# Transposing the feed-forward activations on VectorE and by SBUF to SBUF transfers instead of on TensorE

## The chip, the cores and the metric

The kernel runs on one core of one Trainium2 chip. The time is the device time of one execution in microseconds (us). The kernel before takes 1112.11 us, the median of 3 runs (1111.66 to 1112.41).

## The reference

The first half is attention with normalised queries and keys, over 8 batches, 12 heads, 448 positions and 64 elements per head:

```python
q_n, k_n = rmsnorm(q, g_q), rmsnorm(k, g_k)      # (8, 12, 448, 64)
scores = q_n @ k_n^T / sqrt(64)
attn = exp(scores - max) / (sum + 1e-9)
x = (attn @ v) as (8*448, 12*64)                 # 3584 tokens, 768 wide
```

The second half is a feed-forward block with the SoLU activation and a layer norm:

```python
h = x @ w_in                                     # 768 -> 1024
solu = h * softmax(h)
ln = (solu - mean) / sqrt(var + 1e-6) * g_ln
out = ln @ w_out                                 # 1024 -> 768
```

All is float32, and the two weights arrive as float64 and are converted in the kernel.

## The kernel before, in words

Only `fast_path` runs on these inputs (`general_path`, its twin for large gains, is compiled and skipped). Attention goes by pairs of heads: 8 batches x 6 pairs are 48 steps, n = 0 to 47. The feed-forward goes by tiles of 128 tokens: 28 tiles, t = 0 to 27. The two run interleaved: tile t can begin when the attention of its tokens is done.

What a step n issues, in this order: the loads of pair n+4 (L505, eight transfers on SP, each 32 partitions by 14 pieces of 128 B), the squares of pair n+3, two of the four key chunks of the scores (`s`, L572) with their exponentials (`E`, L576), the transpose of q and k of pair n+1 on VectorE (`qkT`, L559), the norm of pair n+2 (`ss` L529, `nx`, `ny`, and `qkn` on GpSimd, L549), the product with the values of pair n-1 (`o`, L595), the load of v for pair n+1 (L514), the sums of pair n-1 (`sm`, L604, with `es`, the added exponentials), and the last two chunks of scores. `divide` (L617 to L621) turns `o` and `sm` into `xT`, the transposed input of the feed-forward.

What a tile issues: `ff_in` in two halves (`h`, L635, 6 matmuls of 512 columns each), then `ff_max`, `ff_moments` and `ff_norm` (L645 to L667), which leave the normalised activation `u` (128 tokens by 1024), then `ff_transpose`, which needs `u` with the 1024 features on partitions (`uT`, 8 blocks of 128x128), and `ff_out` in two halves (`po`, L686, 8 matmuls of 384 columns each), whose result is copied to `y` (L687) and stored (L689, on ScalarE's queue). `ff_transpose` runs four tiles after the `ff_in` of its tile, so `u` is ready long before.

The order is written out by hand: within `tc.manual_schedule()` every engine executes its instructions in the order in which the program issues them. Pieces of work are called through `unit`, which counts them and lets pieces that were put off by `later` follow one, two or three units on. The feed-forward's pieces stand in the list `events`, for each tile in the order

```python
events += [a, c, b, d, e]    # ff_in(t, 0), ff_transpose(t-4), ff_in(t, 1), ff_out(t-4, 0), ff_out(t-4, 1)
```

and a step takes up to five of them, when the attention is far enough: `ff(0)` after the second chunk of scores, `ff(1)` after `sums`, `ff(2)` after the fourth chunk. The list is not aligned to the steps, so where `ff_transpose` falls changes in the course of the kernel: in tiles 0 to 12 it stands in `ff(0)`, ahead of the values and sums, in tiles 13 to 19 in `ff(1)`, just behind the sums. After the last step the remaining pieces follow without attention work between them; the last four tiles are `ff_transpose`, `ff_out`, `ff_out` four times over.

Weights are converted during the first 22 steps (`convert_w`, the buffer `tmp`); its buffers shared a tag with `uT` (two buffers), so one took the place of the other.

Buffers: `work` and `loads` have two unless said otherwise (`qk` three, `v` three, `u` five), PSUM has one buffer `h` of two banks and six of one bank. SP issues all loads, in program order; a transfer that waits for a buffer holds up those behind it.

Of the kernel before, what the change touches and what calls it, by code (L numbers as in the profile page):

```python
# [9 lines left out]
FP32 = mybir.dt.float32  # L10
U32 = mybir.dt.uint32
# [355 lines left out]
def fast_path(  # L367
# [16 lines left out]
    nc = tc.nc  # L384
    B, H, S, D = q.shape
    DM, DFF = moe_w_in.shape
    P = 128
    NJ = 4
    SP = S // NJ
    NB = S // 32  # L390
    NP = H // 2
    KD = DM // P
    KF = DFF // P
# [6 lines left out]
    loads = ctx.enter_context(tc.tile_pool(name="loads", bufs=2))  # L400
    work = ctx.enter_context(tc.tile_pool(name="work", bufs=2))
    small = ctx.enter_context(tc.tile_pool(name="small", bufs=4))
    ps_h = ctx.enter_context(tc.tile_pool(name="ps_h", bufs=1, space=bass.MemoryType.PSUM))
    ps_t = ctx.enter_context(tc.tile_pool(name="ps_t", bufs=6, space=bass.MemoryType.PSUM))

    ident = consts.tile([P, P], FP32, name="ident")
# [3 lines left out]
    w_out = consts.tile([P, KF, DM], FP32, name="w_out")  # L410
# [46 lines left out]
    def convert_w(step, raw):  # L457

        _, dst, c, cols = step
        n = cols.stop - cols.start  # L460
        lo, hi = raw[:, :, 0], raw[:, :, 1]
        tmp = work.tile([P, 2, n], U32, tag="uT", name="tmp")
        e, m = tmp[:, 0], tmp[:, 1].bitcast(FP32)
        ei = e.bitcast(I32)

        def fields():
            nc.vector.tensor_scalar(tmp[:, 1], hi, 0xFFFFF, None, OP.bitwise_and)  # L467
            nc.vector.tensor_scalar(e, hi, 20, 0x7FF, OP.logical_shift_right, OP.bitwise_and)

        def scale():  # L470
            nc.scalar.activation(m, tmp[:, 1], AF.Copy, scale=2.0 ** -20, bias=1.0)
            nc.scalar.activation(ei, ei, AF.Relu, bias=m896)

        def join():
            nc.vector.scalar_tensor_tensor(m, lo, 2.0 ** -52, m, OP.mult, OP.add)  # L475
            nc.vector.tensor_scalar(ei, ei, 255.0, 2.0 ** 23, OP.min, OP.mult)
            nc.vector.scalar_tensor_tensor(e, hi, 0x80000000, e, OP.bitwise_and, OP.bitwise_or)  # L477

        def product():
            if dst is w_in:  # L480
                nc.gpsimd.tensor_tensor(dst[:, c, cols], m, e.bitcast(FP32), OP.mult)
            else:

                nc.vector.scalar_tensor_tensor(
                    dst[:, c, cols], m, gcol[:, c : c + 1], e.bitcast(FP32), OP.mult, OP.mult
                )

        return [fields, scale, join, product]
# [21 lines left out]
    def load_v(n):  # L510
        b, hp = divmod(n, NP)
        d = st[n]
        d["v"] = loads.tile([SP, 2, NJ, D], FP32, tag="v", name="v", bufs=3)
        nc.sync.dma_start(d["v"], v[b, 2 * hp : 2 * hp + 2].rearrange("h (j p) d -> p h j d", j=NJ))  # L514

    def squares(n):
# [83 lines left out]
    def sums(n):  # L600
        d = st[n]
        d["sm"] = ps_t.tile([P, S], FP32, tag="t", name="sm")
        for h in range(2):
            nc.tensor.matmul(  # L604
                d["sm"][h * D : (h + 1) * D, :], ones[0:SP, :], d["es"][:, h], start=True, stop=True
            )
        later(1, lambda: divide(n))

    def divide(n):

        b, hp = divmod(n, NP)
        d = st[n]
        if b // 2 not in xTs:
            xTs[b // 2] = work.tile([P, KD, 2 * S], FP32, tag="xT", name="xT")
        r = work.tile([P, NB, 32], FP32, tag="r", name="r")
        rc = small.tile([P, NB], FP32, tag="rc", name="rc")
        nc.vector.transpose(r.rearrange("p b i -> p (b i)"), d["sm"])  # L617
        nc.vector.reciprocal(rc, r[:, :, 0])
        nc.vector.transpose(r, rc.rearrange("p b -> p b ()").to_broadcast([P, NB, 32]))  # L619
        c0 = (b % 2) * S  # L620
        nc.vector.tensor_tensor(xTs[b // 2][:, hp, c0 : c0 + S], d["o"], r.rearrange("d b i -> d (b i)"), OP.mult)  # L621
        del st[n]
# [5 lines left out]
    def ff_in(t, half):  # L628
        m, i = divmod(t, 2 * S // P)
        d = mt.setdefault(t, {})  # L630
        if half == 0:
            d["h"] = ps_h.tile([P, DFF], FP32, tag="h", name="h")
        hs = slice(half * 512, half * 512 + 512)
        for c in range(KD):
            nc.tensor.matmul(  # L635
                d["h"][:, hs], xTs[m][:, c, i * P : (i + 1) * P], w_in[:, c, hs], start=(c == 0), stop=(c == KD - 1)
            )
# [29 lines left out]
        nc.vector.tensor_scalar(d["u"], d["u"], d["mv"][:, 0:1], d["e"], OP.subtract, OP.mult)  # L667

    def ff_transpose(t):
        d = mt[t]  # L670
        d["uT"] = work.tile([P, KF, P], FP32, tag="uT", name="uT")
        for half in range(2):
            pt = ps_t.tile([P, 4, P], FP32, tag="t", name="pu")
            for i in range(4):
                c = 4 * half + i
                nc.tensor.transpose(pt[:, i], d["u"][:, c * P : (c + 1) * P], ident)  # L676
            (nc.vector.tensor_copy if half else nc.scalar.copy)(d["uT"][:, 4 * half : 4 * half + 4], pt)  # L677

    def ff_out(t, half):
        d = mt[t]  # L680
        if half == 0:
            d["y"] = work.tile([P, DM], FP32, tag="y", name="y")
        hs = slice(half * HO, (half + 1) * HO)
        po = ps_t.tile([P, HO], FP32, tag="t", name="po")
        for c in range(KF):
            nc.tensor.matmul(po, d["uT"][:, c], w_out[:, c, hs], start=(c == 0), stop=(c == KF - 1))  # L686
        nc.scalar.copy(d["y"][:, hs], po)  # L687
        if half == 1:
            nc.scalar.dma_start(out[t * P : (t + 1) * P, :], d["y"])  # L689
            del mt[t]  # L690
# [37 lines left out]
    def feed():  # L728

        nonlocal wdone  # L730
        for c in list(stages):
            c.pop(0)()
            if len(c) == 1 and len(raws) < len(wq):
                raws.append(load_w(wq[len(raws)]))
            if not c:
                stages.remove(c)
        if wdone < min(wtarget, len(wq)) and len(stages) < 2 and not (stages and len(stages[-1]) > 2):
            stages.append(convert_w(wq[wdone], raws[wdone]))
            wdone += 1
# [5 lines left out]
    def second(t, a, b):  # L745
        return [(W_OUT + 1, lambda: ff_transpose(t)), a, (W_OUT + 1, lambda: ff_out(t, 0)), b, (W_OUT + 1, lambda: ff_out(t, 1))]

    nothing = (0, None)
    for t in range(NT):
        ready = -(-(t + 1) * P // S) * NP + 1  # L750
        a = (max(ready, W_IN + 1), lambda t=t: ff_in(t, 0))
        b = (max(ready, W_IN + 1), lambda t=t: ff_in2(t))
        waiting.append(t)
        if len(waiting) > (LAG if t < NT - 8 else 1):
            c, _, d, _, e = second(waiting.pop(0), nothing, nothing)
# [11 lines left out]
    load(0)  # L767
    setup()
    load_v(0)
    raws.append(load_w(wq[0]))  # L770
    load(1)
    raws.append(load_w(wq[1]))
    load(2)
    load_v(1)
    with tc.manual_schedule():
        prepare(0)
# [17 lines left out]
        for n in range(N):  # L794
# [38 lines left out]
            if n and n + 1 < N:  # L833
                load_v(n + 1)
# [87 lines left out]
```

## Time and profile before

| | |
|---|---|
| median of 3 runs | 1112.11 us |
| profiled execution | 1109.11 us, of it 1107.3 us span from first to last instruction |
| TensorE matmuls (PE) | 1035.3 us busy, 93% |
| TensorE weight loads (PEld, beside PE) | 475.6 us, 43% |
| VectorE (DVE) | 605.4 us, 55% |
| ScalarE (ACT) | 370.6 us, 33% |
| GpSimd (POOL) | 240.3 us, 22% |
| transfers, SP's queue (q1) | 225984 packets, 45.64 MB, 20.9% of 16 engines |
| granted TensorE clock, mean | 0.981 |

How to read it: the page gives for each group of instructions the line, the engine, the operation and the tiles (output <- inputs), the count, the busy time, the mean of one in ns, and the idle time just before with what ended it. The chain of work that ended last is followed back from the last instruction, so it tells what the end waited for. In a timeline a row has the start and the length in us; rows of the same kind are merged, and in square brackets stands how long the engine was idle before and who released it. Matmuls overlap each other, so the length of one record is not what it costs; the chain and the starts of neighbours give that. An fp32 matmul has two records.

### The profile page before, as it was taken

The page shows a single profiled execution, that of the slowest core. Times are in us where ns is not written, and L with a number is a line of the kernel's source. Part 1 is how long each engine was busy: PE and PEld are TensorE (multiplying, and loading weights), DVE is VectorE, ACT ScalarE, POOL GpSimd, SP SyncE. Part 2 cuts the span into 40 slices and gives each one's busy share as a digit, 9 for nine tenths or more (in the row PEclk, how much of TensorE's full clock was granted, in tenths as well). Part 3 has the DMA queues.
Part 4 walks back from the last instruction along what each step waited for, and adds up shares of the span by engine and source line. Part 5 has one row for each costly group of instructions (what it writes and reads, how often), then busy time and mean ns, then how long its engine had stood idle before and what let it go on. Part 6 is the DMA issues. An engine that isn't in the chain of part 4 may idle for free.

```text
span 1107.3 us, 10659 instructions
## 1 busy us (share of the span) xinstructions
PE 1035.3 (93%) x3617; PEld 475.6 (43%) x3617; DVE 605.4 (55%) x1018; ACT 370.6 (33%) x773; POOL 240.3 (22%) x155
## 2 busy tenths in 40 slices
PE   3988888888789999999999999999999999999997
PEld 1323233333234444444444444444444444455554
DVE  3999996569997444444444444454446644522300
ACT  3656553235564222222222222332224322311110
POOL 2565651123223111111111011121112211100000
PEclk9899999998989999999999999999999999999999
DMA  7454544014543111111111111121111100000010
GB/s 140 89 122 98 124 87 85 23 39 93 112 88 62 40 40 40 39 32 33 32 37 40 40 40 39 40 51 40 40 39 40 34 23 24 14 15 15 15 44 31
DMA packets 230391, 57.49 MB, mean 52 GB/s; under 512 B 223152, under 2 KB 223160, under 8 KB 230328
## 3 DMA queue, kind: packets, MB, share of 16 engines
q1 hardware_dynamic: 225984, 45.64, 20.9%
q10 hardware_dynamic: 4344, 11.08, 2.6%
q8 instruction: 30, 0.49, 0.2%
q14 instruction: 33, 0.27, 0.1%
HBM read 45.68 MB, written 11.01 MB: 51 GB/s over the span
## 4 chain that ended last, share of the span: by engine, by line
PE 75%; DVE 14%; issue 4%; ACT 3%; DMA 1%; SPq 1%; ACTq 0%; DVEq 0%
PE po L686 27%; PE h L635 26%; PE s L572 9%; PE o L595 9%; DVE es L586 2%; PE pu L676 2%; PE sm L604 2%; DVE tmp L467 2%; DVE qkT L559 2%; DVE tmp L475 1%; SPq L505 1%; DVE r L619 1%; DVE tmp L477 1%; DVE r L617 1%; PE ss L529 1%
## 5 line engine op out<-in xcount | busy, mean ns | idle before, releaser
L635 PE MATMUL h<-w_in,xT 128*128 128x512 f32 x672 | 305.0, 604 | 11.7 <-DVE u L653 11.7
L686 PE MATMUL po<-w_out,uT 128*128 128x384 f32 x896 | 298.0, 489 | 2.9 <-ACT uT L677 2.9
L686 PEld LDWEIGHTS po<-w_out,uT 128*128 128x128 f32 x896 | 168.3, 190 | 132.9 <-issue 15.0
L572 PE MATMUL s<-qkT 64*112 64x448 f32 x768 | 204.6, 584 | 16.9 <-ACT E L576 6.7
L576 ACT ACTIVATE E<-s 112x448 f32<-112x448 f32 x384 | 178.0, 550 | 110.0 <-PE s L572 109.9
L635 PEld LDWEIGHTS h<-w_in,xT 128*128 128x128 f32 x672 | 126.2, 193 | 167.5 <-issue 162.8
L584 POOL TENSOR_TENSOR es<-E 112x896 f32<-112x896 f32 x48 | 110.5, 2301 | 325.2 <-ACT E L576 318.7
L595 PE MATMUL o<-E,v 112*64 112x448 f32 x768 | 163.9, 572 | 1.2 <-DVE xT L621 1.2
L572 PEld LDWEIGHTS s<-qkT 64*112 64x112 f32 x768 | 76.6, 177 | 136.9 <-issue 73.6
L677 DVE COPY uT<-pu 128x512 f32<-128x512 f32 x28 | 19.2, 687 | 187.3 <-PE pu L676 187.3
L586 DVE TENSOR_TENSOR es<-es,E 112x896 f32<-112x896 f32 x96 | 115.1, 1199 | 10.9 <-ACT E L576 7.8
L663 POOL TENSOR_TENSOR he<-he,mhalf 128x1 f32<-128x1 f32 x28 | 21.7, 774 | 379.2 <-DVE he L662 379.2
L549 POOL TENSOR_TENSOR qkn<-qk,ny 128x896 f32<-128x896 f32 x48 | 83.0, 1730 | 81.6 <-DVE ny L544 35.0
L648 ACT ACTIVATE u<-h,hmax 128x1024 f32<-128x1024 f32 x28 | 31.2, 1114 | 207.3 <-DVE hmax L645 207.3
L687 ACT COPY y<-po 128x384 f32<-128x384 f32 x56 | 26.8, 479 | 213.5 <-PE po L686 213.5
L595 PEld LDWEIGHTS o<-E,v 112*64 112x64 f32 x768 | 53.2, 143 | 86.5 <-issue 80.5
L645 DVE TENSOR_REDUCE hmax<-h 128x1 f32<-128x1024 f32 x28 | 34.3, 1224 | 84.3 <-PE h L635 84.3
L604 PE MATMUL sm<-es,ones 112*64 112x448 f32 x192 | 44.8, 544 | 16.0 <-DVE es L586 14.1
L617 DVE STREAM_TRANSPOSE r<-sm 128x448 f32<-128x448 f32 x48 | 31.0, 646 | 45.8 <-PE sm L604 45.8
L524 DVE TENSOR_REDUCE part<-sq 128x28 f32<-128x896 f32 x48 | 51.7, 1076 | 5.9 <-ACT sq L519 5.9
L519 ACT ACTIVATE sq<-qk 128x896 f32<-128x896 f32 x48 | 45.8, 955 | 23.1 <-ACT y L687 11.3
L559 DVE STREAM_TRANSPOSE qkT<-qkn 128x896 f32<-128x896 f32 x48 | 52.9, 1102 | 0.0
(54 smaller groups left out, 578.7 us busy)
## 6 DMA issues: line engine op xcount, KB each, us to landing
qk<-in_q_dram SPq DMA_DIRECT2D x192, 56.0 KB, 2.6
qk<-in_k_dram SPq DMA_DIRECT2D x192, 56.0 KB, 2.4
v<-in_v_dram SPq DMA_DIRECT2D x48, 224.0 KB, 3.0
out_dram<-y ACTq DMA_DIRECT2D x28, 384.0 KB, 2.3
raw<-in_moe_w_in_dram SPq DMA_DIRECT2D x12, 512.0 KB, 4.2
raw<-in_moe_w_out_dram SPq DMA_DIRECT2D x16, 384.0 KB, 3.4
grow<-in_g_q_dram ACTq DMA_DIRECT2D x2, 0.2 KB
grow<-in_g_k_dram ACTq DMA_DIRECT2D x2, 0.2 KB
```

Source lines behind the costliest of these rows:

```text
L519: nc.scalar.activation(d["sq"], d["qk"].rearrange("p s b d -> p (s b) d"), AF.Square)
L524: nc.vector.tensor_reduce(d["part"], d["sq"], AX, OP.add)
L549: nc.gpsimd.tensor_tensor(d["qkn"], d["qk"].rearrange("p s b d -> p (s b) d"), d["y"].rearrange("p b -> p b ()").to_broadcast([P, 2 * NB, ...
L559: nc.vector.transpose(d["qkT"].rearrange("p s t -> p (s t)"), d["qkn"].rearrange("p b d -> p (b d)"))
L572: nc.tensor.matmul(s, d["qkT"][hh, 1, kc * SP : (kc + 1) * SP], d["qkT"][hh, 0, :], start=True, stop=True)
L576: nc.scalar.activation(d["E"][:, kc, h], d["s", h], AF.Exp)
L584: nc.gpsimd.tensor_tensor(d["es"], d["E"][:, 0], d["E"][:, 1], OP.add)
L586: nc.vector.tensor_tensor(d["es"], d["es"], d["E"][:, kc], OP.add)
L595: nc.tensor.matmul(d["o"][h * D : (h + 1) * D, :], d["v"][:, h, kc], d["E"][:, kc, h], start=(kc == 0), stop=(kc == NJ - 1),)
L604: nc.tensor.matmul(d["sm"][h * D : (h + 1) * D, :], ones[0:SP, :], d["es"][:, h], start=True, stop=True)
L635: nc.tensor.matmul(d["h"][:, hs], xTs[m][:, c, i * P : (i + 1) * P], w_in[:, c, hs], start=(c == 0), stop=(c == KD - 1))
L686: nc.tensor.matmul(po, d["uT"][:, c], w_out[:, c, hs], start=(c == 0), stop=(c == KF - 1))
```

## The change

`ff_transpose` no longer uses TensorE. VectorE transposes `u` in 32x32 blocks into a new buffer `ub`: each block is transposed where it lies, so the features of a block land on the 32 partitions of its token group. Sixteen transfers on SP then move them: from partition group a (tokens) of `ub` to partition group m (features) of `uT`, each 32 partitions by 8 pieces of 128 B, 32 KB. The eight transposes a tile, their two PSUM tiles and the two copies to SBUF go. The place of `ff_transpose` in the list of events is the same.

To make room, `ub` shares the tag `tmp` with the weight conversion, `uT` has its own, and three buffer counts go down: `v` from three to two, `r` and `y` from two to one. `ff_out` reads the same data of `uT` in the new shape.

```diff
@@ convert_w
-        tmp = work.tile([P, 2, n], U32, tag="uT", name="tmp")
+        tmp = work.tile([P, 2, n], U32, tag="tmp", name="tmp")
@@ load_v
-        d["v"] = loads.tile([SP, 2, NJ, D], FP32, tag="v", name="v", bufs=3)
+        d["v"] = loads.tile([SP, 2, NJ, D], FP32, tag="v", name="v", bufs=2)
@@ divide
-        r = work.tile([P, NB, 32], FP32, tag="r", name="r")
+        r = work.tile([P, NB, 32], FP32, tag="r", name="r", bufs=1)
@@ ff_transpose
         d = mt[t]
-        d["uT"] = work.tile([P, KF, P], FP32, tag="uT", name="uT")
-        for half in range(2):
-            pt = ps_t.tile([P, 4, P], FP32, tag="t", name="pu")
-            for i in range(4):
-                c = 4 * half + i
-                nc.tensor.transpose(pt[:, i], d["u"][:, c * P : (c + 1) * P], ident)
-            (nc.vector.tensor_copy if half else nc.scalar.copy)(d["uT"][:, 4 * half : 4 * half + 4], pt)
+        ub = work.tile([P, KF, 4, 32], FP32, tag="tmp", name="ub")
+        d["uT"] = work.tile([P, KF, 4, 32], FP32, tag="uT", name="uT")
+        nc.vector.transpose(ub.rearrange("p c m t -> p (c m t)"), d["u"])
+        for a in range(4):
+            for m in range(4):
+                nc.sync.dma_start(
+                    d["uT"][m * 32 : m * 32 + 32, :, a], ub[a * 32 : a * 32 + 32, :, m]
+                )
@@ ff_out
-            d["y"] = work.tile([P, DM], FP32, tag="y", name="y")
+            d["y"] = work.tile([P, DM], FP32, tag="y", name="y", bufs=1)
@@
-            nc.tensor.matmul(po, d["uT"][:, c], w_out[:, c, hs], start=(c == 0), stop=(c == KF - 1))
+            nc.tensor.matmul(po, d["uT"][:, c].rearrange("p a t -> p (a t)"), w_out[:, c, hs], start=(c == 0), stop=(c == KF - 1))
```

## Prediction

> **What bounds the kernel now.** I read the busy table first, then the chain of work that ended last, then the timelines around the change. The page:
>
> ```profile
> span 1107.3 us, 10659 instructions
> PE 1035.3 (93%) x3617; PEld 475.6 (43%) x3617; DVE 605.4 (55%) x1018; ACT 370.6 (33%) x773; POOL 240.3 (22%) x155
> ...
> PE po L686 27%; PE h L635 26%; PE s L572 9%; PE o L595 9%; DVE es L586 2%; PE pu L676 2%; PE sm L604 2%; DVE tmp L467 2%; DVE qkT L559 2%; DVE tmp L475 1%; SPq L505 1%; DVE r L619 1%; DVE tmp L477 1%; DVE r L617 1%; PE ss L529 1%
> ...
> L677 DVE COPY uT<-pu 128x512 f32<-128x512 f32 x28 | 19.2, 687 | 187.3 <-PE pu L676 187.3
> ...
> qk<-in_q_dram SPq DMA_DIRECT2D x192, 56.0 KB, 2.6
> ```
>
> TensorE is the limit: once the feed-forward runs (from about 340 us) there is next to no gap on it. The transposes (pu, L676) hold 2% of the chain, about 22 to 28 us; that is all the change can win. VectorE waits 187 us in front of its copy L677, so there is room on it, but the groups don't say when. So I looked tile by tile: where can VectorE begin the new transpose, and when does TensorE want uT for po (L686)? VectorE runs in order, so the start is where the copy L677 stands, without its wait for pu. The 28 tiles fall into four kinds. A tile of the first kind (tile 8), VectorE's timeline:
>
> ```profile
> 577.27 0.69 DVE L677 COPY uT<-pu 128x512 f32<-128x512 f32 x1 [9.86 <-PE pu L676]
> ```
>
> VectorE had been free for 9.86 us, since 567.41; po of this tile starts at 586.33. Slack 18.9 us. It is so for tiles 1 to 12 (18.3 to 20.7). A tile of the second kind (tile 13), first VectorE's timeline, then the chain:
>
> ```profile
> 737.78 0.62 DVE L621 TENSOR_TENSOR xT<-o,r 128x448 f32<-128x448 f32 x1
> 738.32 0.68 DVE L677 COPY uT<-pu 128x512 f32<-128x512 f32 x1
> ```
> ```profile
> 735.34 0.75 PE sm L604 x4
> 736.10 1.02 PE pu L676 x8
> 737.12 5.15 PE h L635 x12
> 742.27 1.69 PE s L572 x8
> 743.96 1.17 PE po L686 x3
> ```
>
> Here the copy waits for no pu: it stands behind xT (L621), which hangs on sm. VectorE can begin at 738.32, and the timeline starts po at 743.89: slack 5.6 us. It is the same in tiles 13 to 19. This is the place that decides. Tile 0 has 7.7 us, tile 20 has 9.0, tiles 21 to 23 have 14. The last four have no other work between their transposes and po; TensorE's timeline:
>
> ```profile
> 1052.35 1.04 PE L676 MATMUL pu<-ident,u 128*128 128x128 f32 x8
> 1054.08 10.59 PE L686 MATMUL po<-w_out,uT 128*128 128x384 f32 x32 [0.69 <-ACT uT L677]
> 1064.50 1.04 PE L676 MATMUL pu<-ident,u 128*128 128x128 f32 x8
> 1066.23 10.59 PE L686 MATMUL po<-w_out,uT 128*128 128x384 f32 x32 [0.69 <-ACT uT L677]
> ```
>
> 12.2 us per tile, 1.6 of them for pu and the copy.
>
> How dear a burst of transfers on SP is, its timeline shows at one pair's loads (eight transfers of 32 partitions by 14 pieces of 128 B; the new ones are 32 by 8 pieces of 128 B):
>
> ```profile
> 732.74 1.88 SPq L505 DMA_DIRECT2D qk<-in_q_dram  x4
> 734.65 2.05 SPq L505 DMA_DIRECT2D qk<-in_k_dram  x4
> ```
>
> Issues are in series: 0.36 us to the second, then 0.52 from one to the next.
>
> **The Trainium skill.** "VectorE: DVE Perf Modes", section "The three transpose paths", says that VectorE transposes 32x32 blocks each by itself and not 128x128 at once; hence the 16 transfers. The trace gives the price: 1102 ns for 128x896 (L559). "DMA: Bandwidth & Descriptors", section "Issuing engines are not separate DMA queues", calls the time to start a DMA "usually small relative to the DMA itself". The trace disagrees for this size: 16 issues at about 0.5 us are 8 us beside 2.4 us from issue to landing. Its section "Rules for kernel authors" says that under 64 KB one pays mostly overhead. The trace agrees: a 56 KB load lands in 2.4 us though its 448 packets take 448 x 12.5 ns / 16 = 0.35 us of sixteen engines.
>
> **The change part by part.**
>
> Removed from TensorE: 8 transposes a tile. Their records say 273 ns each, but they overlap; the chain gives 0.91 us a tile in tiles 1 to 12 (1.02 in 13 to 19, 0.87 in 21 to 23). Removed from ScalarE and VectorE: the copies (0.59 and 0.69 us a tile), both off the path outside the last four tiles.
>
> Added, from the start on VectorE to po, call it X:
> - Transpose of 128x1024: 1.102 x 1024/896 = 1.26 us. Its waits for the transfers that last read the buffer ub (two buffers, so those of two tiles before, long done): 0.1, an estimate; 0 to 0.4.
> - Hand over to SP: 0.03 to 0.05 (POOL's qkn ends at 581.66, SP issues at 581.69).
> - 16 issues: 0.36 + 14 x 0.50 = 7.36 us to the start of the last. The pitch: issues behind a transfer with 448 pieces come at 0.52, behind one with 896 at 0.60 (v at 17.58, next at 18.18); so 0.50 for 256. Bounds: 0.36 for each (5.4) and 0.52 plus one wait for a semaphore (8.2).
> - Landing of the last: no SBUF to SBUF transfer is in the trace. Loads take 1.7 at least, 2.4 in the median; I take 2.1, bounds 1.6 and 2.6.
> - TensorE's po waits for eight DMA semaphores: 0.1, bounds 0 and 0.3.
> X = 1.26 + 0.1 + 0.05 + 7.36 + 2.1 + 0.1 = 11.0 us; bounds 8.4 and 12.4.
>
> What lies on the path:
> - Tiles 1 to 12: 11.0 is under 18.9, hidden by o, sm and h; gain 12 x 0.91 = 10.9. If that cover were gone each would cost as below.
> - Tiles 13 to 19: 738.32 + 11.0 = 749.32 against 743.89: 5.4 later, 7 x 5.4 = +38.0. TensorE has no other idle time in these steps to give it back (29.0 of 29.0 us busy between 732 and 761), and what follows on it is ready.
> - Tile 0: 342.18 + 11.0 = 353.2 against 349.92: +3.3. Tile 20: 968.56 + 11.0 = 979.6 against 977.54: +2.0.
> - Tiles 21 to 23: 11.0 under 14.1; gain 3 x 0.87 = 2.6.
> - Tile 24: VectorE free at 1049.4, so po at 1060.4 against 1054.08: +6.35. Tiles 25 to 27: po back to back at 10.55 instead of 12.2: -1.65 x 3 = -4.95. Their uT has two buffers: transfers for tile 26 start when po of 24 ends, and 0.05 + 7.36 + 2.1 + 0.1 = 9.6 is under 10.5, just hidden. Sum +1.4.
> Total: -10.9 + 38.0 + 3.3 + 2.0 - 2.6 + 1.4 = +31.2 us.
>
> Queues. On SP the 16 issues stand behind the pair's loads (and v in tiles 13 to 19), which wait for POOL's qkn and for o of the pair before last; both are done before VectorE ends (735.3 for o, 739.6 for VectorE in tile 13). Behind them the next pair's loads wait: from 732.7 to about 747.5 in tile 13; squares needs them in the step after next, near 785, so nothing. The listing of the new kernel's instructions with their waits shows that every transfer, the stores on ACT too, takes one of eight semaphores in turn and waits for its last user: eight issues are 4.0 us and a landing is 2.4, so no wait; in tiles 24, 26 and 27 one transfer waits for the store of an earlier tile (out of 23 lands near 1055.4, the 13th issue is near 1056.7). v with two buffers, r and y with one: v is reloaded after o two pairs earlier, a step ahead of use; r is used by VectorE in order; y's store lands 2.3 us after issue, under the 5.2 us to the next copy. All nothing, at worst 2 us. VectorE gets 28 x 1.26 instead of 28 x 0.69: 16 us more, in its idle time. Transfers: 28 x 4096 packets x 12.5 ns / 16 = 90 us of the sixteen engines, 8% on 23%.
>
> The profiled execution took 1109.11 (span 1107.3 and 1.8 around it), 3.0 below the median 1112.11. With +31.2 it would be 1140.3, and the median 1143.3.
>
> **Rivals.**
> (a) The burst is cheaper. This is the one that ends faster. Each tile of 13 to 19 pays X - 5.57, tile 0 X - 7.74, the tail X - 9.6, against 13.5 gained elsewhere and 0.7 in tile 20: the sign turns at X = 7.8 us. For: some issues take only 0.31 and the fastest landing is 1.7. Against: in every burst of loads the third and later issues come at 0.52; X = 7.8 would need 16 issues at 0.31 throughout. At X = 7.2 the sum is 11.4 - 0.5 - 0.7 - 2.4 - 13.5 = -5.7: 1106.4. Near that point, X = 7.8: 1112.
> (b) Bound by bound, X = 8.4 to 9.5: 7 x 2.9 to 7 x 3.9 and the rest give +5 to +16: 1117 to 1128.
> (c) SBUF to SBUF pieces of 128 B move slowly and set the pitch at about 0.8: X = 16. Tiles 13 to 19 +73, tiles 0 and 20 +15, tiles 21 to 23 +5, the tail +13, less 10.9: +95, 1207. Against: loads of the same piece size take 12.5 ns a packet. For: nothing in the trace, it just has no such transfer.
> (d) Everything is hidden, gain 27 us, 1085: would need VectorE to start tiles 13 to 19 before xT, and its order forbids it. No chance worth a number.
>
> **How the numbers follow.** Likeliest case (X of 9.5 to 12.4) 0.80: 1143, its own range 1128 to 1160. (b) 0.05, (c) 0.08, (a) 0.07, of which 0.02 within 0.2% of the median (about what a measurement of this kernel can tell from no change) and 0.05 faster. Slower is 0.80 + 0.05 + 0.08 = 0.93. The range takes the likeliest case and part of (b): 1120 to 1160.
>
> **What would show it.** In the new profile: idle time of TensorE before po released by a DMA on uT, some 6 us in each of tiles 13 to 19 (5.4 and the 1.02 that pu no longer takes), 4 in tile 0, 3 in tile 20, 8 in tile 24, none in tiles 1 to 12; the VectorE transpose at 1.26 us; 16 issues spread over 7 to 8 us; landings near 2.1. It is wrong if the issues come at 0.36, if SP holds the burst back behind a load or v, or if TensorE waits for uT in tiles 1 to 12.

## The result and the profile after

The changed kernel takes 1190.89 us (median of 4 runs, 1188.48 to 1193.74) against 1112.05 for the kernel before in the same runs: ratio 1.071, 95% interval [1.0685, 1.0735]. It is slower by 79 us, where 31 were forecast; it lies above the forecast's range of 1120 to 1160. The profiled execution took 1193.74 us, of it a span of 1191.9.

The page of the kernel after, with the busy row of TensorE, its granted clock over the span in 40 slices (9 is full), the chain by line, po's group (busy, mean ns, then idle time before it), and the new transfers (count, KB each, us from issue to landing):

```profile
span 1191.9 us, 10860 instructions
...
PE 1039.0 (87%) x3393; PEld 465.6 (39%) x3393; DVE 626.7 (53%) x1018; ACT 355.3 (30%) x745; POOL 240.4 (20%) x155
...
PEclk9999998987898999999999999888989888989989
...
PE po L689 25%; PE h L635 23%; PE o L595 7%; PE s L572 7%; SPq L678 5%; DVE es L586 3%; DVE qkT L559 2%; PE sm L604 2%; DVE tmp L467 2%; DVE r L619 1%; SPq L505 1%; DVE r L617 1%; DVE tmp L475 1%; DMA uT<-ub 1%; DVE hmax L645 1%
...
L689 PE MATMUL po<-w_out,uT 128*128 128x384 f32 x896 | 323.1, 521 | 84.0 <-DVE qkT L559 42.7
...
uT<-ub SPq DMA_DIRECT2D x448, 32.0 KB, 1.9
```

The clock row and po's group of the kernel before, for comparison:

```profile
PEclk9899999998989999999999999999999999999999
L686 PE MATMUL po<-w_out,uT 128*128 128x384 f32 x896 | 298.0, 489 | 2.9 <-ACT uT L677 2.9
```

Three things are new. The issues on SP (SPq L678) stand on the chain with 5%. TensorE is idle for 84 us before po, where it was 3. And po's matmuls, which are the same, are longer: 521 ns in the mean against 489, and the clock row falls to 8 again and again in the second half, where it stayed at 9 before; e4 below shows that these two belong together. (The page names qkT as what ended most of the idle time; at tile 13 that instruction had ended at 753.75, 0.2 us before po, and has nothing to do with po. Of the nine semaphores that po waits for, the page names one; the DMAs are the late ones, as the experiments show.)

Tile 13, the kind that decides, on TensorE in the kernel before, and then on TensorE, VectorE and SP in the changed kernel:

```profile
743.89 10.59 PE L686 MATMUL po<-w_out,uT 128*128 128x384 f32 x32
```
```profile
743.61 1.76 PE L572 MATMUL s<-qkT 64*112 64x448 f32 x8
753.95 12.77 PE L689 MATMUL po<-w_out,uT 128*128 128x384 f32 x32 [8.57 <-DVE qkT L559]
```
```profile
740.02 0.62 DVE L621 TENSOR_TENSOR xT<-o,r 128x448 f32<-128x448 f32 x1
740.75 1.25 DVE L675 STREAM_TRANSPOSE ub<-u 128x1024 f32<-128x1024 f32 x1
```
```profile
742.02 10.39 SPq L678 DMA_DIRECT2D uT<-ub  x16
752.52 2.10 SPq L505 DMA_DIRECT2D qk<-in_q_dram  x4
```

VectorE starts at 740.75, po at 753.95: X, the time from the start on VectorE to po, is 13.2 us, not 11.0. Of these 10.39 are the sixteen issues. The last issue alone takes 0.61, so the pitch (the time from one issue to the next) is (10.39 - 0.61) / 15 = 0.65 us. Then po takes 12.77 us for the 32 records that took 10.59 before. A stretch of the kernel before in the same place, then one of the changed kernel:

```profile
732.00:761.00 29.00, 29.00 (x102) 14.06 (x102) 12.68 (x22) 8.13 (x17) 4.13 (x3) 1.00 0.18 41
```
```profile
740.00:780.00 40.00, 31.43 (x96) 14.51 (x95) 14.72 (x23) 7.54 (x16) 5.12 (x3) 0.87 0.20 41
```

(columns: stretch, length, busy time of PE, PEld, DVE, ACT, POOL, granted clock, DMA share, GB/s). The clock is 0.87, where it was 1.00. In tile 8, of the covered kind, TensorE goes from h to po without a gap:

```profile
586.95 5.42 PE L635 MATMUL h<-w_in,xT 128*128 128x512 f32 x12
592.20 5.32 PE L689 MATMUL po<-w_out,uT 128*128 128x384 f32 x16
```

Where the time came from, by the start of sm (L604) of each pair in the traces, and for the last row to the end of the last po, each against the kernel before, in us. The last column is experiment e4, explained below:

| stretch | forecast | after | e4, the waits filled |
|---|---|---|---|
| before the first transpose of u | 0 | +2.2 | +3.9 |
| tile 0 (pair 22 to 23) | +3.3 | +10.0 | +5.9 |
| tiles 1 to 12 (pair 23 to 34, 11 steps) | -10.0 | -10.0 | -10.0 |
| tiles 13 to 19, seven steps | +38.0 | +69.8 | +53.7 |
| tiles 20 to 27 | +0.8 | +13.7 | +8.7 |

(The forecast's -10.9 is 12 tiles; 11 of them lie between these marks.)

### The profile page after: what moved, and what is told of

It is laid out like the page before. It is cut to its first block, busy times and chain, and to the rows that moved or that the text cites. A ratio compares the mean times of both kernels' runs of the same rounds, so it can differ in the third digit from the quotient of the medians.

```text
span 1191.9 us, 10860 instructions
## 1 busy us (share of the span) xinstructions
PE 1039.0 (87%) x3393; PEld 465.6 (39%) x3393; DVE 626.7 (53%) x1018; ACT 355.3 (30%) x745; POOL 240.4 (20%) x155
## 4 chain that ended last, share of the span: by engine, by line
PE 65%; DVE 18%; issue 6%; SPq 6%; ACT 2%; DMA 1%; POOL 1%; ACTq 0%; DVEq 0%; POOLq 0%
PE po L689 25%; PE h L635 23%; PE o L595 7%; PE s L572 7%; SPq L678 5%; DVE es L586 3%; DVE qkT L559 2%; PE sm L604 2%; DVE tmp L467 2%; DVE r L619 1%; SPq L505 1%; DVE r L617 1%; DVE tmp L475 1%; DMA uT<-ub 1%; DVE hmax L645 1%
## 5 line engine op out<-in xcount | busy, mean ns | idle before, releaser
L689 PE MATMUL po<-w_out,uT 128*128 128x384 f32 x896 | 323.1, 521 | 84.0 <-DVE qkT L559 42.7
L689 PEld LDWEIGHTS po<-w_out,uT 128*128 128x128 f32 x896 | 180.7, 204 | 229.2 <-issue 65.2
L537 DVE TENSOR_SCALAR nx<-ss 128x28 f32<-128x28 f32 x48 | 8.7, 182 | 243.5 <-ACT ny L536 243.5
L604 PE MATMUL sm<-es,ones 112*64 112x448 f32 x192 | 44.9, 544 | 16.5 <-DVE es L586 14.5
```

Of the source, the lines that this page charges most:

```text
L604: nc.tensor.matmul(d["sm"][h * D : (h + 1) * D, :], ones[0:SP, :], d["es"][:, h], start=True, stop=True)
L689: nc.tensor.matmul(po, d["uT"][:, c].rearrange("p a t -> p (a t)"), w_out[:, c, hs], start=(c == 0), stop=(c == KF - 1))
```

## The experiments

My theory after the result, A: the price is sixteen issues in series on SP, which the order of the events leaves uncovered (no other work of TensorE hides them) in tiles 0, 13 to 20 and 24 on. Rival B: the price is moving 128 B pieces within SBUF, whoever issues them. And C, for the longer matmuls: the wait itself makes the clock fall.

**e1, half of the issues on ScalarE's queue.**

```diff
-                nc.sync.dma_start(
+                (nc.scalar if m % 2 else nc.sync).dma_start(
```

> The changed kernel, with every second of the sixteen transfers issued on ScalarE's queue instead of SP's; all data still move. Theory A (the issues in series on SP are the cost: 0.65 us each, 16 in a row): 8 issues take 5.2 us instead of 10.4, X in tiles 13 to 19 falls from 13.2 to about 8.2, TensorE's wait there from 8.5 to about 3.5 us, and with the shorter waits the half-clock spells go too: about 1125 us. Theory B (moving 128 B pieces from SBUF to SBUF is the cost, whoever issues): X stays near 13 and the time near 1190.

Measured: 1168.97 us, ratio 1.0504 [1.0483, 1.0524]. In tiles 13 to 19 issues, X and waits are as A has them. SP's timeline and VectorE's start at tile 13, then TensorE's at tiles 13 to 15:

```profile
739.77 5.17 SPq L678 DMA_DIRECT2D uT<-ub  x8
```
```profile
738.50 1.25 DVE L675 STREAM_TRANSPOSE ub<-u 128x1024 f32<-128x1024 f32 x1
```
```profile
746.96 10.56 PE L689 MATMUL po<-w_out,uT 128*128 128x384 f32 x32 [3.84 <-DMA qk<-in_q_dram]
779.14 12.25 PE L689 MATMUL po<-w_out,uT 128*128 128x384 f32 x32 [3.41 <-DMA uT<-ub]
813.10 12.25 PE L689 MATMUL po<-w_out,uT 128*128 128x384 f32 x32 [3.50 <-DMA uT<-ub]
```

The same bytes in the same pieces, and X is 8.5 us (738.50 to 746.96): B falls. (The load of q that the page names for the first wait is not read by po; it is a name as misleading as qkT above.) The seven steps cost 28 us instead of 70. The time of 1125 was missed elsewhere: the last tiles cost 33.6 us. ScalarE runs in order, so there its eight issues stand behind the copies of y and the store of the tile before, and each po waits again:

```profile
1098.29 0.48 ACT L690 COPY y<-po 128x384 f32<-128x384 f32 x1 [4.68 <-PE po L689]
1098.80 0.34 ACTq L692 DMA_DIRECT2D out_dram<-y  x1
1099.33 5.94 ACTq L678 DMA_DIRECT2D uT<-ub  x8
```

The three po above also show the edge of C, and a second part of the miss: I had expected the spells of half clock to go with the shorter waits. Of the seven waits of 3.4 to 3.8 us in tiles 13 to 19 five are still followed by a spell of 3.4 us at half clock and a po of about 12.25 us, two are not (10.56).

**e2, pieces of 1 KB instead of 128 B.**

```diff
-        ub = work.tile([P, KF, 4, 32], FP32, tag="tmp", name="ub")
-        d["uT"] = work.tile([P, KF, 4, 32], FP32, tag="uT", name="uT")
-        nc.vector.transpose(ub.rearrange("p c m t -> p (c m t)"), d["u"])
+        ub = work.tile([P, 4, 32, KF], FP32, tag="tmp", name="ub")
+        d["uT"] = work.tile([P, 4, 32, KF], FP32, tag="uT", name="uT")
+        nc.vector.transpose(ub.rearrange("p m t c -> p c m t"), d["u"].rearrange("p (c m t) -> p c m t", m=4, t=32))
...
```

> The changed kernel with the free dimensions of ub and uT reordered so that each of the sixteen transfers has 32 pieces of 1 KB instead of 256 of 128 B; same bytes, same result. TensorE then loads its weights with a stride of 32 B, which may cost by itself. If the pitch of 0.65 us is a price per transfer between SBUF partitions (theory A, fixed), it stays at 0.65 and X near 13. If it follows the number of pieces (theory A, by pieces), it falls towards 0.45 and X towards 10, the time towards 1145 to 1160. If moving the pieces is the cost (theory B), the landing of 1.9 us gets shorter as well.

Measured: 1199.01 us, ratio 1.0771 [1.0753, 1.0789]. SP at tile 13:

```profile
744.11 10.01 SPq L678 DMA_DIRECT2D uT<-ub  x16
```

The pitch is 0.63 us with an eighth of the pieces, and the landing stays at 1.9: it is not the pieces. The 8 us more fit the strides, though no run takes these alone: VectorE's transpose takes about 2.0 us instead of 1.2 when it writes with a stride, and a weight load of po 313 ns instead of 190.

**e3, the smaller buffers alone, with the transposes of before.**

```diff
-        d["v"] = loads.tile([SP, 2, NJ, D], FP32, tag="v", name="v", bufs=3)
+        d["v"] = loads.tile([SP, 2, NJ, D], FP32, tag="v", name="v", bufs=2)
-        r = work.tile([P, NB, 32], FP32, tag="r", name="r")
+        r = work.tile([P, NB, 32], FP32, tag="r", name="r", bufs=1)
-            d["y"] = work.tile([P, DM], FP32, tag="y", name="y")
+            d["y"] = work.tile([P, DM], FP32, tag="y", name="y", bufs=1)
```

> The kernel before (TensorE transposes) with only the three smaller buffer counts of the change: v two, r one, y one. The changed kernel was about 2 us late before the first transpose of u. If the buffers are the cause: 1114 us, the loss before 340 us. If not: 1112 us, within 1.

Measured: 1112.2 us, ratio 0.999 [0.9978, 1.0002]: the buffers cost nothing that the medians show. Its profiled execution was 4.6 us late at pair 22, with the median unchanged, and e7 below, which has all buffers of before, was 3.4 late there. The start of the kernel differs by some us between executions, so the +2.2 of the first row of the table need not be an effect of the change.

**e4, the waits filled with matmuls of no use.**

```diff
+        fill = {0: 8, 20: 5, 24: 10}.get(t, 9 if 13 <= t <= 19 else 0)
+        if half == 0 and fill:
+            pf = ps_t.tile([P, 512], FP32, tag="t", name="pf")
+            for i in range(fill):
+                nc.tensor.matmul(pf, w_in[:, 0, 0:P], w_in[:, 1, 0:512], start=True, stop=True)
```

> The changed kernel with matmuls of no use put on TensorE just ahead of po in tiles 0, 13 to 19, 20 and 24 (8, 9, 5 and 10 of 512 columns, about 0.86 us each), so that the wait for uT is filled with work. Transfers and order are unchanged. Theory C (the wait of over 8 us halves the granted TensorE clock for 7 to 10 us, which makes po 2.3 us longer each time): the half-clock spells in tiles 13 to 19 go, each of these steps is 7.6 us longer than before instead of 9.98, and the time falls by about 20 us to 1170. Rival (these 2.35 us a step are part of the wait itself): the time stays at 1190.

Measured: 1169.91 us, ratio 1.0515 [1.0497, 1.0533], 21 us faster for 172 more matmul records. TensorE at tile 13:

```profile
742.85 7.99 PE L691 MATMUL pf<-w_in 128*128 128x512 f32 x18
751.53 10.56 PE L694 MATMUL po<-w_out,uT 128*128 128x384 f32 x32 [0.69 <-DVE qkT L559]
```
```profile
742.00:780.00 38.00, 37.31 (x118) 16.75 (x114) 14.69 (x23) 7.63 (x17) 5.11 (x3) 1.00 0.22 44
```

po is back at 10.56 us, the clock in the stretch is 1.00, and each of the seven steps is 7.4 to 7.8 us longer than before, which is X minus slack, 13.2 - 5.6 = 7.6. C holds: 16 of the 70 us of tiles 13 to 19 are the clock. The clock records of the changed kernel give the same by another way: in these seven tiles 32.6 us of half clock fall on po, and half of that is 16.3.

**e5, the transpose of each tile one tile ahead.**

```diff
-            events += [a, c, b, d, e]
+            ahead = second(waiting[0], nothing, nothing)[0]
+            events += ([a, c, b] if t == LAG else [a, b]) + [d, e, ahead]
...
-    for t in waiting:
-        events += [x for x in second(t, nothing, nothing) if x[1]]
+    for i, t in enumerate(waiting):
+        _, _, d, _, e = second(t, nothing, nothing)
+        ahead = [second(waiting[i + 1], nothing, nothing)[0]] if i + 1 < len(waiting) else []
+        events += ahead + [d, e]
```

> The changed kernel with ff_transpose of each tile moved one tile ahead in the list of events: behind ff_out of the tile before, so that VectorE's transpose and the sixteen transfers have a whole tile's work to hide behind. Nothing else is changed. Theory A (the latency X of 13.2 us from VectorE's start to po, in places where the order gives it only 5 to 9 us): no wait of TensorE for uT and no half-clock spells in tiles 0 to 23, 24 x 0.91 = 22 us less than the kernel before in that part; in the last four tiles the transfers (16 x 0.65 + 1.9 + about 0.2 = 12.5 us) are longer than po (10.5), so there about 12.5 us a tile against 12.2 before, and somewhat more where a transfer waits for the semaphore of a store: 1092 to 1098 us. Rival (the transfers cost TensorE something of their own, by sharing SBUF or by po's eight semaphore waits): above 1112.

Measured: 1114.58 us, ratio 1.0025 [1.0015, 1.0035]. 76 us are gone without a transfer less: the latency stayed, its cover came. But the sum is not A's 1092 to 1098; by the number alone it falls on the rival's side (above 1112). The steps speak against the rival: the seven that cost 70 us now gain 0.83 us each against the kernel before. What is lost is lost in three places. Two were not foreseen and are seen more plainly in e6. The third is the last four tiles, which lose 7.4 us where about 1 was expected, with waits as in the changed kernel:

```profile
1062.46 23.08 PE L689 MATMUL po<-w_out,uT 128*128 128x384 f32 x64 [9.85 <-DMA uT<-ub]
```

**e6, as e5, with tiles 24 to 27 transposed on TensorE.**

```diff
...
+        if t >= NT - 4:
+            uT = d["uT"].rearrange("p c a t -> p c (a t)")
+            for half in range(2):
...
+                    nc.tensor.transpose(pt[:, i], d["u"][:, c * P : (c + 1) * P], ident)
...
+            return
```

> As e5, but tiles 24 to 27, which have no other work to hide behind, are transposed on TensorE as in the kernel before, one tile ahead. Theory A: tiles 0 to 23 gain 22 us as in e5, the last four gain the 0.7 us that po waited for the copies: about 1087 us, below both kernels. Rival as for e5: above 1112.

Measured: 1105.0 us, ratio 0.994 [0.9924, 0.9955]. That is 0.6% below the kernel before, but 18 us above the expectation. One loss is tile 0, which the edit had left in its old place (6.7 us). The other lies at pairs 40 to 42, in steps that have no feed-forward work. SP, ScalarE and TensorE there:

```profile
841.12 10.71 SPq L687 DMA_DIRECT2D uT<-ub  x16
851.96 2.08 SPq L505 DMA_DIRECT2D qk<-in_q_dram  x4
854.09 2.04 SPq L505 DMA_DIRECT2D qk<-in_k_dram  x4
```
```profile
858.11 0.95 ACT L519 ACTIVATE sq<-qk 128x896 f32<-128x896 f32 x1 [6.66 <-DMA qk<-in_k_dram]
858.97 1.83 ACT L576 ACTIVATE E<-s 112x448 f32<-112x448 f32 x4
```
```profile
859.54 1.76 PE L604 MATMUL sm<-es,ones 112*64 112x448 f32 x4 [3.60 <-ACT E L576]
```

The burst of tile 17 holds SP for 10.7 us, the loads of q and k behind it come late, ScalarE waits 6.66 us for them in front of its squares, the exponentials stand behind the squares, and TensorE waits. In a step of 29 us the loads have time; in one of 8 to 14 us they have none.

**e7, the control: the kernel before with the same move.** The edit is that of e5 on the old transposes.

> The control for e5 and e6: the kernel before, TensorE transposes and all, with the same move of ff_transpose one tile ahead. If the gain of e5 and e6 comes from taking the transposes off TensorE, this one stays near 1112, less about 3 us for the waits of po in the last four tiles: 1109. If the move itself is what gains, it comes down as far as e6, 1087.

Measured: 1109.48 us, ratio 0.9969 [0.9958, 0.998], as expected: the move by itself gains 3 us, and not the 25 that would bring it to 1087.

**e8, the source in HBM.**

```diff
-                    d["uT"][m * 32 : m * 32 + 32, :, a], ub[a * 32 : a * 32 + 32, :, m]
+                    d["uT"][m * 32 : m * 32 + 32, :, a], q[a, m].rearrange("(b t) (x d) -> x t b d", t=32, x=2)[0][:, 0:KF]
```

> The changed kernel with the source of the sixteen transfers replaced by a piece of q in HBM, of the same shape (32 partitions by 8 pieces of 128 B); VectorE still transposes into ub, but what it leaves there is not used, so the output is not the reference's. Only the pitch of the issues is asked. If the 0.65 us comes from the source being SBUF, the pitch falls to the 0.52 of the loads of q and k or a little below. If it comes from the count of issues in a row, or from the destination, it stays at 0.65.

SP's timeline in a tile of the covered kind (one execution):

```profile
472.01 7.87 SPq L678 DMA_DIRECT2D uT<-in_q_dram  x16
```

(7.87 - 0.45) / 15 = 0.495 us from issue to issue. With the same shape and destination, the SBUF source makes it 0.65. Over all 448 issues the median of one is 0.449 us long here and 0.609 in the changed kernel, so it is the issue itself that is longer. This kernel leaves out the transposed data, and its transfers do not wait for VectorE (at tile 13 they begin at 732.10, 2.6 us before the transpose), so its 1109.47 us do not price the source.

**e9, as e6, without its two losses:** tile 0 ahead as well, tile 17 on TensorE (the edit is shown against e6).

```diff
-            events += ([a, c, b] if t == LAG else [a, b]) + [d, e, ahead]
+            events += [a, b, d, e, ahead]
+        elif t == LAG - 1:
+            events += [a, b, second(waiting[0], nothing, nothing)[0]]
...
-        if t >= NT - 4:
+        if t == 17 or t >= NT - 4:
```

> As e6, with its two remaining losses taken away: tile 0 is transposed one tile ahead too (in e6 it stood where the change put it, and TensorE waited 5.5 us there), and tile 17, whose burst stood on SP ahead of the loads of q and k of a step without feed-forward work (squares waited 6.7 us for them, and TensorE behind), is transposed on TensorE like the last four. If these two are the causes: 6.7 and 6.6 us less than e6, 1092 us, about 2% below the kernel before. If not, about 1105.

Measured: 1088.21 us, ratio 0.9774 [0.9761, 0.9788], better than both kernels. Its page:

```profile
span 1087.8 us, 10830 instructions
...
L698 PE MATMUL po<-w_out,uT 128*128 128x384 f32 x896 | 296.8, 489 | 0.0
```

No idle time before po, the mean back at 489 ns. It lies 21 us below e7, which has nearly the same order (tile 0 apart) and TensorE's transposes for all tiles. 23 tiles without them at the 0.91 us of the prediction come to 20.9, an estimate that fits.

**e10, four wide transfers instead of sixteen.**

```diff
-            for m in range(4):
-                nc.sync.dma_start(
-                    d["uT"][m * 32 : m * 32 + 32, :, a], ub[a * 32 : a * 32 + 32, :, m]
-                )
+            nc.sync.dma_start(d["uT"][:, :, a], ub[:, :, a])
```

> The changed kernel with four transfers a tile of all 128 partitions each instead of sixteen of 32; the bytes, the 1024 pieces of 128 B and the place are the same, but nothing moves between partition groups, so the output is not the reference's. Theory A (the count of issues): X = 1.24 + 3 x 0.65 + about 2.2 for the landing = 5.4 us, TensorE waits at most 1 us in tiles 13 to 19, the clock stays full, and the kernel is below the one before: 1095 to 1105 us. Theory B (moving the pieces): X hardly changes, the time stays above 1150.

Measured: 1097.81 us, ratio 0.9865 [0.985, 0.988]. SP, VectorE and TensorE at tile 13:

```profile
731.34 2.79 SPq L677 DMA_DIRECT2D uT<-ub  x4
```
```profile
730.08 1.23 DVE L675 STREAM_TRANSPOSE ub<-u 128x1024 f32<-128x1024 f32 x1
```
```profile
736.03 10.56 PE L686 MATMUL po<-w_out,uT 128*128 128x384 f32 x32 [1.15 <-DMA uT<-ub]
```

Same bytes, same pieces of 128 B (4096 a tile; the 1024 of the expectation are those of one transfer), in the place of the change: X is 5.95 us (730.08 to 736.03) and the wait 1.15. The count of issues is what costs, 0.70 us each here. A tile cannot be brought into place with these four; the run only prices the count.

## Why the prediction was wrong

**What held.** The way: slower. The four kinds of tiles and the place that decides. The gain of 0.91 us a tile in tiles 1 to 12, hidden behind o, sm and h, to the hundredth. The transpose at 1.26 us (1.22 in the mean, 1.25 at tile 13). The buffers at nothing, and the eight semaphore waits of po at little (0.25 us from the last landing to po, where 0.1 was put). The waits on SP behind loads and v at nothing, in the places where the change put the burst.

**The term that was mis-sized: the pitch.** "16 issues: 0.36 + 14 x 0.50 = 7.36 us to the start of the last", with 0.52 as the upper bound. Measured: 15 x 0.65 = 9.8 us. I took the pitch from loads out of HBM and argued that it falls with fewer pieces. e8 shows that the figure was right for an HBM source (0.495) and e2 that pieces hardly matter (0.63 with an eighth of them); what makes it 0.65 is the SBUF source, for which the trace of before had no row. The landing was 1.9 instead of 2.1. So X is 1.27 + 9.78 + 1.9 + 0.25 = 13.2 instead of 11.0, above my upper bound of 12.4 (whose terms add up to 12.8). With 13.2 in the sums of the prediction tiles 13 to 19 come to +53.4 instead of 38.0, which e4 measures as 53.7, and the whole to -10.9 + 53.4 + 5.5 + 4.2 - 2.6 + 8.0 = +57.6 us. The last term is tile 24 at +8.6 and three tiles at 12.0 us instead of 12.2. The runs measured 79.

**The step that was missing: the clock.** "what follows on it is ready", and I priced it at full speed. In the seven steps each wait of 8.2 to 8.6 us brought a spell of 6.8 or 10.2 us at half clock. It begins 2.7 to 5.0 us into the wait and reaches 2.8 to 6.2 us into po, so that po at tile 13 took 12.77 instead of 10.59 us. The spell at tile 13 (the third number from the right is the clock):

```profile
748.30:758.30 10.00, 4.35 (x7) 2.52 (x8) 4.91 (x9) 0.00 (x0) 1.34 (x1) 0.50 0.44 72
```

The Trainium skill says so: "TensorE: Matmul & The Clock Gate", section "Part 1: The HAM clock gate", has the clock at half after an idle window of about 3.4 us, in windows that run freely. The trace agrees for the long waits: each of the ten over 4.9 us in the kernel after has its spell of 6.8 or 10.2 us. The runs don't confirm 3.4 us as a limit, though: waits of 1.96 us (tile 26 of the kernel after), 2.05 and 2.72 us (e8) were followed by a spell of 3.4 us, and one of 3.84 us (e1) by none; where they differ, the measurement decides. e4 prices the spells: 16 us in tiles 13 to 19, about 4 in tile 0 and 5 in the last eight. (These come from one profiled execution of each kernel; by the medians e4 gains 21.) That is what the sum of +57.6 lacks. Even with the right pitch the forecast would have missed this: it had waits of some 6 us, and in tile 20 a wait of 4.95 us was enough for a spell of 6.8 us.

The record had it. In its steady part the kernel before has no wait over 1 us, but in its first 340 us, which I didn't read for this, three waits of 3.91 us each have a spell of 3.4 us at half clock at their end. The first of them, and the clock behind it:

```profile
183.01 7.08 PE L635 MATMUL h<-w_in,xT 128*128 128x512 f32 x12 [3.91 <-DVE u L653]
```
```profile
183.70:187.00 3.30, 3.30 (x5) 1.24 (x5) 1.90 (x6) 0.00 (x0) 0.55 (x1) 0.50 0.21 34
```

The same twelve records take 5.32 us at tile 13. The clock row, 9 throughout the steady part, was a condition that I took for a constant.

**The last four tiles.** "just hidden" stood on 9.6 us against 10.5. With the true pitch it is 12.0 from free buffer to uT: po of tile 24 begins 8.3 us later than the steps before explain (forecast 6.35), and the 4.95 us that tiles 25 to 27 should give back are eaten by waits and half clock:

```profile
1139.03 23.39 PE L689 MATMUL po<-w_out,uT 128*128 128x384 f32 x64 [9.76 <-DMA uT<-ub]
1164.39 22.57 PE L689 MATMUL po<-w_out,uT 128*128 128x384 f32 x64 [1.96 <-DMA uT<-ub]
```

Two tiles take 23 us where they take 21 at full clock.

**The rivals.** (a) and (b) needed a cheaper burst; it was dearer. (c), pitch 0.8 from slow pieces, had the side right and the cause wrong: neither the pieces nor the SBUF to SBUF movement is slow (e2: the same landing of 1.9 us with 1 KB pieces), only the issue. The measured time lies near its 1207, but by another way: X is 13.2 and not 16, and the clock, which it does not have, adds 21 us.

**Open.** Why an issue with an SBUF source takes 0.15 us longer is not settled; the runs show only that it goes with the source. What decides whether a wait of 2 to 4 us brings a spell isn't settled either. Whether other splits of the burst over the two queues would help in the ahead order wasn't tried.

## What to carry to other kernels

A step that is moved off the bounding engine is paid in latency, so count it from the point where its input is ready to the point where it is wanted, tile by tile, and move its start ahead (e5: 76 us from the order alone) before judging it. Many small transfers cost their issues in series, about half a microsecond each out of HBM and 0.65 to 0.7 out of SBUF here, for 32 to 128 KB each, and everything behind them on that queue is late by the burst. Price a new wait of TensorE of several us above its own length: here 8.5 us of waiting cost 10.8, waits of 3.4 to 3.8 us cost 1.7 more in five of seven cases, and waits of about 1.1 us (e10) nothing more. Look for such waits and their clock in the whole trace, not only in the steady part.

## What the runs showed that was not expected

- The issue pitch depends on the source: 0.495 us from HBM, 0.63 to 0.65 from SBUF with 32 partitions, 0.70 with 128.
- VectorE's transpose of 128x1024 takes 1.22 us into a dense buffer and 2.02 us when its output has a stride of 32 B; a weight load with that stride takes 313 ns instead of 190.
- A wait of TensorE of as little as 2.0 us can be followed by 3.4 us at half clock (two of seven waits of 2.0 to 2.7 us in e8).
- Work of no use on TensorE made the kernel 21 us faster (e4).
